# Softmax sums taken another way in the first block, epsilon added as a bias, and attention spread over fewer steps

## The chip, the cores and the metric

The kernel runs on one core of one Trainium2 chip. Its engines are TensorE (PE, with its weight loads shown apart as PEld), VectorE (DVE), ScalarE (ACT), GpSimd (POOL) and SyncE (SP), which here only issues transfers. Each engine works through its own queue in order. The metric is the device time of one execution in microseconds; lower is better.

## The reference

Attention with a soft cap, then a feed-forward layer with a squared ReLU, then a soft mixture of experts. All of it is float32 in the inputs' values, apart from two weight matrices that arrive as float64.

```python
scores = scale * np.matmul(q, k.transpose(0, 1, 3, 2))      # (4, 12, 448, 448)
scores = cap * np.tanh(scores / cap)
scores = scores - np.max(scores, axis=-1, keepdims=True)
attn = np.exp(scores)
attn = attn / (np.sum(attn, axis=-1, keepdims=True) + 1e-09)
x = np.matmul(attn, v)                                      # to (1792, 768)
r = np.maximum(x @ w_in, 0.0)                               # (1792, 2048)
x = (s * (r * r) + b) @ w_out                               # (1792, 768)
logits = x @ phi                                            # (1792, 32)
d = softmax(logits, axis=0); c = softmax(logits, axis=1)
slot_out[e] = np.maximum((d.T @ x)[e] @ w1[e], 0.0) @ w2[e] # 8 experts, 4 slots
out = c @ slot_out
```

## The kernel before

The four batches are four blocks. For each batch, attention is worked out for twelve heads in three groups of four (a quad, `Q` in the code, 0 to 11 over the run), and the result, split into a high and a low part, is the tile `x` of 448 columns that the block's first matrix product (`hidden`, tile `hp`) reads. Scores stand transposed: a chunk is 112 of the 448 key positions on partitions, so a quad has four chunks. One call of `scores` makes the scores of two heads for one chunk (tile `sc`, six matmuls, two PSUM tiles in the first stage and one afterwards) and the tanh into tile `e`; after the second pair of heads `expo` takes the exponential of the whole chunk in place. `e` has three buffers.

The softmax's denominators are sums over partitions, made on PE by a matmul with ones into tile `Sm`; the numerators times `v` go into tile `U`, of which there is one. `finish` takes the reciprocal of the sums, multiplies `U` by it and splits the product into `x`. Constant 1e-9 is scaled by exp(-cap) first, because the maximum is not subtracted where the cap is small enough (the fast branch, which runs here).

Two ways of summing stand beside each other. In the first block (quads 0 to 2, `Q < DIRECT`) all four chunks go through the ones matmul, and a fifth set of four matmuls adds tile `es`, whose partitions 0 to 111 are zero and whose partition 112 holds epsilon (lines 168 and 172). From quad 3 on, DVE adds the four chunks into `es` first (line 158), and only that is summed by matmul, row 112 giving epsilon. GpSimd fills `es` at the start (lines 217 to 222).

`attention` is a generator of 16 steps a quad. Scores are issued on even steps, the other work at fixed steps (`between`, and the four steps of the next quad that end the one before). `run` takes 52 steps of it before any other work (the first stage, up to about 77 us), and then each of the first three blocks takes the 48 steps of the next batch's attention between its own: a block has 48 places, and attention's steps are spread over the first `48 - LEAD` of them (line 671). Meanwhile `convert` turns the float64 weights into float32: a load into one of two `raw` buffers, a scaling copy on ACT, three bit operations on DVE, a store. The last block has no attention; the experts' weights are loaded during it, and the tail after it is paced by those loads. The framework's scheduler may reorder instructions of an engine beyond the order in which the code emits them; a single PSUM tile, tag `T`, is shared in turn by `Sm` (from quad 3 on), `pp`, `tw`, `pf` and `tp`.

## Time and profile before

| | us |
|---|---|
| median of three executions | 686.54 |
| their range | 683.52 to 688.51 |
| the profiled execution | 687.23 |
| its span, first to last instruction | 685.4 |
| PE busy in it | 628.2 (92%) |
| ACT busy | 425.0 (62%) |
| DVE busy | 333.5 (49%) |
| POOL busy | 12.4 (2%) |

The span is shorter than the execution by 1.8 us that lie around the instructions. Busy shares are means over stages that have different limits, so each stage has to be read for itself. The granted PE clock, 1.00 for full speed and 0.50 for half, is 0.98 over the span. Matmuls on float32 data are recorded as two passes each, so that 48 of them in the code are 96 records.

### The profile page before, as it was taken

The numbers are of one execution on the slowest core, as the hardware profiler recorded it, in microseconds if no ns is written. First come the engines' busy times: TensorE is split into PE (matmuls) and PEld (weight loads), VectorE is DVE, ScalarE is ACT, GpSimd is POOL, SyncE is SP. The second block draws the span as 40 slices with busy tenths as digits, with TensorE's granted clock in tenths as the row PEclk, the third lists the DMA queues.
The fourth block names the chain that finished last, engine by engine and source line by source line (L and its number), as shares of the span: only waits on it lengthen the run. The fifth ranks groups of instructions, "written<-read, shape, count | busy, mean of one in ns | idle before, by whom it ended". The sixth has DMA issues, their size and how long they took to land.

```text
span 685.4 us, 11531 instructions
## 1 busy us (share of the span) xinstructions
PE 628.2 (92%) x4714; PEld 395.7 (58%) x4714; DVE 333.5 (49%) x482; ACT 425.0 (62%) x693; POOL 12.4 (2%) x14
## 2 busy tenths in 40 slices
PE   3898999999999899999999999999999988997753
PEld 1333556656566465565665665666868863346643
DVE  6773587896973763555352744534432223111211
ACT  4997889887887776677776777775655551000101
POOL 6000000000000000000000000000000000000000
PEclk9999999999999999999999999999999998998996
DMA  8654367578595532132232221211967629999996
GB/s 250 224 201 119 119 230 266 175 247 280 181 307 192 182 103 81 47 100 74 74 106 63 82 77 63 60 48 45 369 262 286 265 107 403 419 419 418 418 398 212
DMA packets 43724, 136.62 MB, mean 199 GB/s; under 512 B 4352, under 2 KB 21264, under 8 KB 36752
## 3 DMA queue, kind: packets, MB, share of 16 engines
q1 hardware_dynamic: 43376, 135.28, 55.2%
q8 instruction: 39, 0.64, 0.4%
q0 software_dynamic: 288, 0.53, 0.2%
q14 instruction: 21, 0.17, 0.1%
HBM read 117.70 MB, written 18.09 MB: 198 GB/s over the span
## 4 chain that ended last, share of the span: by engine, by line
PE 71%; DMA 12%; ACT 9%; DVE 3%; issue 2%; SPq 0%; DVEq 0%; ACTq 0%
PE hp L438 32%; PE U L189 10%; DMA wt<-in_w_dram 9%; PE sc L115 8%; PE tp L453 4%; ACT e L118 3%; ACT e L153 3%; DMA raw<-in_w_outT_dram 3%; PE hps L732 2%; PE pt L527 2%; PE L L467 2%; PE tw L387 2%; PE pp L369 1%; PE Sm L172 1%; PE si_ps L711 1%
## 5 line engine op out<-in xcount | busy, mean ns | idle before, releaser
L438 PE MATMUL hp<-x,ws 128*128 128x448 f32 x1152 | 278.5, 381 | 0.2 <-ACT ws L422 0.2
L438 PEld LDWEIGHTS hp<-x,ws 128*128 128x128 f32 x1152 | 204.7, 188 | 61.4 <-issue 46.0
L423 DVE TENSOR_TENSOR ws<-wr,ws 128x384 fp32r<-128x384 f32 x128 | 70.6, 554 | 115.3 <-ACT ws L422 114.9
L118 ACT ACTIVATE e<-sc,c_tsc 112x896 f32<-112x896 f32 x96 | 95.9, 1008 | 18.3 <-PE sc L115 17.7
L189 PE MATMUL U<-e,v 112*32 112x448 f32 x768 | 91.0, 542 | 0.2 <-DVE x L75 0.2
L422 ACT CAST ws<-wr 128x384 fp32r<-128x384 f32 x128 | 64.9, 511 | 36.9 <-PE hp L438 36.9
L153 ACT ACTIVATE e<-e,c_acap 112x1792 f32<-112x1792 f32 x48 | 86.2, 1795 | 0.8
L115 PE MATMUL sc<-qh,kh 64*112 64x448 f32 x192 | 46.9, 457 | 13.1 <-DVE kh L74 7.3
L455 ACT COPY g<-tp 112x256 f32<-112x256 f32 x128 | 42.1, 376 | 20.8 <-PE tp L453 20.1
L443 ACT ACTIVATE r<-hp 128x448 f32<-128x448 f32 x64 | 34.6, 540 | 26.9 <-PE hp L438 26.7
L189 PEld LDWEIGHTS U<-e,v 112*32 112x32 f32 x768 | 25.0, 109 | 44.9 <-issue 42.7
L158 DVE TENSOR_TENSOR es<-es,e 112x1792 f32<-112x1792 f32 x18 | 36.4, 2023 | 23.7 <-ACT e L153 23.7
L115 PEld LDWEIGHTS sc<-qh,kh 64*112 64x112 f32 x192 | 18.2, 174 | 46.2 <-issue 22.1
L115 PE MATMUL sc<-ql,kh 64*112 64x448 f32 x192 | 41.5, 384 | 3.2 <-DVE ql L75 3.2
L754 PE MATMUL so_ps<-wt,free 128*32 128x128 f32 x768 | 29.4, 290 | 15.8 <-DMA wt<-in_w_dram 15.8
L775 ACT COPY wt<-op 128x512 f32<-128x512 f32 x12 | 7.0, 586 | 56.7 <-PE op L770 56.7
L115 PE MATMUL sc<-qh,kl 64*112 64x448 f32 x192 | 40.8, 379 | 0.0
L453 PE MATMUL tp<-c_cst,r 128*112 128x128 f32 x256 | 39.0, 275 | 1.3 <-ACT r L444 1.2
L178 DVE RECIPROCAL rec<-rec 128x448 f32<-128x448 f32 x9 | 26.6, 2951 | 24.5 <-ACT rec L177 24.5
L444 ACT ACTIVATE r<-r 128x448 f32<-128x448 f32 x64 | 37.3, 583 | 0.4
L453 PEld LDWEIGHTS tp<-c_cst,r 128*112 128x112 f32 x256 | 29.4, 133 | 11.9 <-ACT g L455 2.4
L754 PEld LDWEIGHTS so_ps<-wt,free 128*32 128x32 f32 x768 | 23.6, 116 | 20.6 <-DMA wt<-in_w_dram 19.6
(141 smaller groups left out, 588.6 us busy)
## 6 DMA issues: line engine op xcount, KB each, us to landing
wt<-in_w_dram SPq DMA_DIRECT2D x48, 1024.0 KB, 15.4
wr<-wsc SPq DMA_DIRECT2D x48, 384.0 KB, 3.1
raw<-in_w_in_dram SPq DMA_DIRECT2D x16, 768.0 KB, 5.2
raw<-in_w_outT_dram SPq DMA_DIRECT2D x16, 768.0 KB, 5.8
wsc<-wr SPq DMA_DIRECT2D x16, 384.0 KB, 3.4
osc<-o SPq DMA_DIRECT2D x24, 256.0 KB, 2.8
wt<-osc SPq DMA_DIRECT2D x6, 1024.0 KB, 7.0
v<-in_v_dram SPq DMA_DIRECT2D x24, 224.0 KB, 3.2
```

What stands on the lines that cost most here:

```text
L115: nc.tensor.matmul(sc[:, i, :S], k[r, c * CP:(c + 1) * CP], q[r, :], start=(n == 0), stop=(n == 2))
L118: nc.scalar.activation(self.e[Q][c][:, 2 * j:2 * j + 2, :], sc[:, :, :S], AF.Tanh, scale=self.c["tsc"][:CP])
L153: self.nc.scalar.activation(e, e, AF.Exp, scale=self.c["acap"][:CP])
L158: self.nc.vector.tensor_add(es, e[0] if c == 1 else es, e[c])
L189: nc.tensor.matmul(self.U[32 * i:32 * i + 32, h, :S], self.v[2 * Q + i // 2][:, i % 2, k * D + 32 * h:k * D + 32 * h + 32], self.chunk(4 * ...
L422: self.nc.scalar.copy(hi, u)
L423: self.nc.vector.tensor_sub(lo, u, hi.bitcast(F32))
L438: nc.tensor.matmul(hp[:, :S], ws[kc // 3][:, w, kc % 3, :], x[:, s, kc, :], start=(k == 0), stop=(k == 3 * KC - 1))
L444: self.mark = nc.scalar.activation(r2, r2, AF.Square).ins
L453: self.nc.tensor.transpose(tp[:CP, q * P:(q + 1) * P], r2[:, q * CP:(q + 1) * CP], self.c["idn"])
L455: self.nc.scalar.copy(self.g[q][:CP, :, fc * P:(fc + 1) * P], tp[:CP, 2 * q * P:2 * (q + 1) * P].rearrange("p (a b) -> p a b", b=P))
L754: nc.tensor.matmul(so_ps[32 * e:32 * e + 32, G, :], ht[G][:, f, 32 * e:32 * e + 32], w2[e // 2][:, e % 2, f, :], start=(f == 0), stop=(f = ...
```

## The change

Epsilon is no longer a row of the summed tile. The sums are copied out of PSUM by an ACT instruction that adds it as a bias, in the first block too, where the reciprocal read PSUM directly; `es` shrinks to 112 partitions and GpSimd fills nothing. In the first block DVE now adds chunks 0 to 2 into `es`, and the matmul with ones runs over `es` and chunk 3 (8 matmuls a quad where there were 20). `U` is accumulated there chunk by chunk, at steps 7, 11 and 15 and at step 3 of the next quad, where it was two chunks at step 9 and two at step 3. `Sm` of the first block moves from a PSUM tile of its own to the shared one. `LEAD` goes from 4 to 10: attention's 48 steps are spread over the first 38 places of a block, not 44.

```diff
--- before.py
+++ after.py
@@ -36,9 +36,9 @@
 EPS = 1e-9
 CAP_FAST = 40.0
 STEPS = 8
-DIRECT = NQ
+LAST = 3
 CASTS = NP
-LEAD = 4
+LEAD = 10
 U = 256
 CU = 768
 XPOS = (1, 4, 7, 10, 13, 15, 15, 15)
@@ -154,29 +154,21 @@
 
     def add(self, Q, c):
 
-        es, e = self.es[:CP], self.e[Q]
-        self.nc.vector.tensor_add(es, e[0] if c == 1 else es, e[c])
-
-    def sums(self, Q, chunks):
+        es, e = self.es, self.e[Q]
+        if c < (LAST if Q < NQ else NCH):
+            self.nc.vector.tensor_add(es, e[0] if c == 1 else es, e[c])
+
+    def sums(self, Q):
 
         nc, c = self.nc, self.c
-        direct = Q < DIRECT
-        if chunks[0] == 0 or not direct:
-            self.Sm = self.psl.tile([P, 512], F32, tag="L", bufs=1, name="Sm") if direct else self.bank("Sm")
-        for k in chunks if direct else ():
+        Sm = self.bank("Sm")
+        parts = [self.es] + self.e[Q][LAST if Q < NQ else NCH:]
+        for n, part in enumerate(parts):
             for i in range(4):
-                nc.tensor.matmul(self.Sm[32 * i:32 * i + 32, :S], c["ones"][:CP, :32], self.chunk(4 * Q + i, k), start=(k == 0), stop=False)
-        if chunks[-1] != NCH - 1:
-            return
-        for i in range(4):
-            nc.tensor.matmul(self.Sm[32 * i:32 * i + 32, :S], c["ones"][:CP + 1, :32], self.es[:CP + 1, i, :], start=not direct, stop=True)
-        rec = self.ap.tile([P, S], F32, tag="rec", bufs=1, name="rec")
-        if Q < NQ:
-            nc.vector.reciprocal(rec, self.Sm[:, :S])
-        else:
-            nc.scalar.copy(rec, self.Sm[:, :S])
-            nc.vector.reciprocal(rec, rec)
-        self.rec = rec
+                nc.tensor.matmul(Sm[32 * i:32 * i + 32, :S], c["ones"][:CP, :32], part[:, i, :], start=(n == 0), stop=(n == len(parts) - 1))
+        self.rec = self.ap.tile([P, S], F32, tag="rec", bufs=1, name="rec")
+        nc.scalar.activation(self.rec, Sm[:, :S], AF.Identity, bias=self.eps)
+        nc.vector.reciprocal(self.rec, self.rec)
 
     def weighted(self, Q, chunks):
 
@@ -214,12 +206,11 @@
         self.prep_pair(0)
         self.prep_pair(1)
         self.load_v(1)
-        self.es = self.ap.tile([P, 4, S], F32, name="es")
-        self.nc.gpsimd.memset(self.es, EPS)
-        if not self.general:
-            self.nc.gpsimd.tensor_scalar(self.es, self.es, self.c["eps"], None, op0=ALU.mult)
-        if DIRECT:
-            self.nc.gpsimd.memset(self.es[:CP], 0.0)
+        self.es = self.ap.tile([CP, 4, S], F32, name="es")
+        self.eps = self.c["eps"]
+        if self.general:
+            self.eps = self.ap.tile([P, 1], F32, name="eps")
+            self.nc.vector.memset(self.eps, EPS)
         last = B * NQ
         for Q in range(last + 1):
             for s in range(2 * STEPS):
@@ -230,13 +221,12 @@
                         if j:
                             self.expo(Q, c)
                     self.between(Q, s)
-                if not self.general and Q and s in (1, 3) and not (s == 1 and Q - 1 < DIRECT):
-                    if s == 1:
-                        self.add(Q - 1, 3)
-                    else:
-                        self.sums(Q - 1, (2, 3))
-                        self.weighted(Q - 1, (2, 3))
-                        self.finish(Q - 1)
+                if not self.general and Q and s == 1:
+                    self.add(Q - 1, 3)
+                if not self.general and Q and s == 3:
+                    self.sums(Q - 1)
+                    self.weighted(Q - 1, (3,) if Q - 1 < NQ else (2, 3))
+                    self.finish(Q - 1)
                 yield
 
     def between(self, Q, s):
@@ -253,17 +243,17 @@
             self.prep_pair(2 * Q + 3)
         if self.general:
             if s == 14:
-                for k in range(1, NCH) if Q >= DIRECT else ():
+                for k in range(1, NCH):
                     self.add(Q, k)
-                self.sums(Q, range(NCH))
+                self.sums(Q)
                 self.weighted(Q, range(NCH))
                 self.finish(Q)
         else:
-            if s == 9:
-                if Q < DIRECT:
-                    self.sums(Q, (0, 1))
+            if Q < NQ and s in (7, 11, 15):
+                self.weighted(Q, (s // 4 - 1,))
+            elif Q >= NQ and s == 9:
                 self.weighted(Q, (0, 1))
-            if s in (9, 13) and Q >= DIRECT:
+            if s in (9, 13):
                 self.add(Q, 1 if s == 9 else 2)
 
     def convert(self, units):
```

What the scheduler makes of it is seen at three places. On PE in the first stage, in quad 2, before (`sc` scores, `Sm` sums, `U` weighted values; the names after the arrow are what is read):

```order
L168 MATMUL Sm<-e,c_ones 32x448 x4
L189 MATMUL U<-e,v 32x448 x8
L115 MATMUL sc<-qh,kh 112x448 x2
L115 MATMUL sc<-ql,kh 112x448
L168 MATMUL Sm<-e,c_ones 32x448 x4
L189 MATMUL U<-e,v 32x448 x8
L115 MATMUL sc<-ql,kh 112x448
L115 MATMUL sc<-qh,kl 112x448 x2
```

The same place after:

```order
L115 MATMUL sc<-qh,kh 112x448 x2
L181 MATMUL U<-e,v 32x448 x16
L115 MATMUL sc<-ql,kh 112x448 x2
L115 MATMUL sc<-qh,kl 112x448 x2
L181 MATMUL U<-e,v 32x448 x8
```

The two sets of sums, each of which stood ahead of scores, are gone from here; `U` still stands inside a group of scores.

On ACT at the end of the first stage, from the second pair of casts of the later quads to the first weight split of block 0, before (L153 is the exponential, L118 the tanh, L74 a cast for a split):

```order
L74 CAST qh<-q_578 128x448
L153 ACTIVATE e<-e,c_acap 112x1792
L118 ACTIVATE e<-sc,c_tsc 112x896 x2
L389 COPY o<-tw 128x512
L153 ACTIVATE e<-e,c_acap 112x1792
L74 CAST qh<-q_661 128x448
L74 CAST kh<-k_662 128x448
L389 COPY o<-tw 128x512
L74 CAST x_385<-U 128x896
```

And after:

```order
L153 ACTIVATE e<-e,c_acap 112x1792
L74 CAST qh<-q_641 128x448
L118 ACTIVATE e<-sc,c_tsc 112x896 x2
L74 CAST kh<-k_642 128x448
L153 ACTIVATE e<-e,c_acap 112x1792
L170 ACTIVATE rec<-Sm,c_eps 128x448
L360 COPY c_tmp<-pp 128x256
L379 COPY o<-tw 128x512
L118 ACTIVATE e<-sc,c_tsc 112x896
L74 CAST x_373<-U 128x896
```

The first exponential of each listing is the last of quad 2. Afterwards the copy of its sums stands behind the next quad's first exponential, with the casts for `q` and `k` ahead of that.

On PE where block 1 starts, before, twelve and more products into its first tiles:

```order
L438 MATMUL hp<-x_1151,ws 128x448 x2
L115 MATMUL sc<-qh,kh 112x448 x2
L115 MATMUL sc<-ql,kh 112x448 x2
L115 MATMUL sc<-qh,kl 112x448 x2
L115 MATMUL sc<-qh,kh 112x448 x2
L115 MATMUL sc<-ql,kh 112x448 x2
L115 MATMUL sc<-qh,kl 112x448 x2
L369 MATMUL pp<-o,c_misc 32x256 x6
```

The like place after is in the last products of block 0, where the scheduler has drawn forward the first scores of block 1's steps:

```order
L115 MATMUL sc<-qh,kl 112x448 x2
L115 MATMUL sc<-qh,kh 112x448 x2
L115 MATMUL sc<-ql,kh 112x448 x2
L115 MATMUL sc<-qh,kl 112x448 x2
L181 MATMUL U<-e,v 32x448
L115 MATMUL sc<-qh,kh 112x448
L359 MATMUL pp<-o,c_misc 32x256 x6
L428 MATMUL hp<-x_373,ws 128x448 x3
```

Two groups of scores stand back to back in both, now in the block before. Over blocks 0 to 2 the products `hp` stand in 135 runs before and 126 after; from block 3 on the rows of PE are the same.

## Rows read from the trace of the kernel before

**Rows 1.** Busy time by stretch: span, PE, PEld, DVE, ACT, POOL, granted clock, DMA share, GB/s.

```profile
12.00:77.00 65.00, 58.76 (x485) 23.09 (x481) 39.38 (x49) 57.73 (x58) 1.36 (x1) 1.00 0.53 179
77.00:212.00 135.00, 132.55 (x830) 82.14 (x829) 105.13 (x135) 111.92 (x169) 0.00 (x0) 1.00 0.71 239
212.00:489.00 277.00, 272.64 (x1730) 173.00 (x1729) 136.36 (x176) 198.40 (x340) 0.60 (x1) 0.99 0.28 92
```

**Rows 2.** Timeline, first 12 us, several engines: start, duration, what, [idle before <-releaser].

```profile
6.68 5.03 POOL L220 TENSOR_SCALAR es<-es,c_eps 128x1792 f32<-128x1792 f32 x1
...
5.18 1.65 DVE L74 CAST qh<-c_tmp 128x448 fp32r<-128x448 f32 x1 [0.59 <-DMA c_tmp<-in_qT_dram]
...
7.04 3.85 DVE L75 TENSOR_TENSOR ql<-c_tmp,qh 128x448 fp32r<-128x448 f32 x1
10.81 0.61 DVE L75 TENSOR_TENSOR kl<-c_tmp,kh 128x448 fp32r<-128x448 f32 x1
...
7.24 0.93 SPq L281 DMA_DIRECT2D raw<-in_w_in_dram  x2
...
7.87 0.56 ACT L74 CAST kh<-c_hh 128x448 fp32r<-128x448 f32 x1 [0.93 <-DMA c_hh<-in_kT_dram]
12.23 1.01 ACT L118 ACTIVATE e<-sc,c_tsc 112x896 f32<-112x896 f32 x1 [3.80 <-PE sc L115]
```

**Rows 3.** Transfers issued in the first 20 us: size, median us to landing.

```profile
raw<-in_w_in_dram SPq DMA_DIRECT2D x2, 768.0 KB, 7.8
```

**Rows 4.** Timeline of ACT, the first stage: first scaling, four idle stretches, one exponential.

```profile
16.98 0.89 ACT L286 ACTIVATE wr<-raw 128x768 f32<-128x768 f32 x1
...
23.79 1.01 ACT L118 ACTIVATE e<-sc,c_tsc 112x896 f32<-112x896 f32 x1 [0.69 <-PE sc L115]
...
46.95 1.91 ACT L118 ACTIVATE e<-sc,c_tsc 112x896 f32<-112x896 f32 x2 [1.35 <-PE sc L115]
...
56.29 1.01 ACT L118 ACTIVATE e<-sc,c_tsc 112x896 f32<-112x896 f32 x1 [1.22 <-PE sc L115]
...
64.72 1.01 ACT L118 ACTIVATE e<-sc,c_tsc 112x896 f32<-112x896 f32 x1 [3.14 <-PE sc L115]
...
70.00 1.80 ACT L153 ACTIVATE e<-e,c_acap 112x1792 f32<-112x1792 f32 x1
```

**Rows 5.** Groups by line, whole span: busy us, mean ns | idle before.

```profile
L168 PE MATMUL Sm<-e,c_ones 112*32 112x448 f32 x96 | 11.5, 551 | 3.0 <-ACT e L153 2.8
L158 DVE TENSOR_TENSOR es<-es,e 112x1792 f32<-112x1792 f32 x18 | 36.4, 2023 | 23.7 <-ACT e L153 23.7
L177 ACT COPY rec<-Sm 128x448 f32<-128x448 f32 x9 | 4.8, 531 | 8.9 <-PE Sm L172 8.9
L485 ACT ACTIVATE c_tmp<-L,c_s 128x448 f32<-128x448 f32 x4 | 2.5, 634 | 4.0 <-PE L L467 4.0
```

**Rows 6.** Timeline, end of the first stage, DVE, ACT and PE.

```profile
73.63 2.96 DVE L175 RECIPROCAL rec<-Sm 128x448 f32<-128x448 f32 x1 [2.86 <-PE Sm L172]
...
77.32 1.09 DVE L199 TENSOR_TENSOR U<-U,rec 128x896 f32<-128x896 f32 x1
...
78.99 0.91 ACT L74 CAST x<-U 128x896 fp32r<-128x896 f32 x1
...
79.93 1.09 DVE L75 TENSOR_TENSOR x<-U,x 128x896 fp32r<-128x896 f32 x1 [0.47 <-ACT x L74]
...
80.37 1.49 PE L438 MATMUL hp<-x,ws 128*128 128x448 f32 x6
...
82.59 2.73 PE L438 MATMUL hp<-x,ws 128*128 128x448 f32 x12
```

**Rows 7.** Timeline of PE, start of block 1: the first of two waits.

```profile
225.12 0.46 PE L115 MATMUL sc<-qh,kh 64*112 64x448 f32 x2 [1.60 <-ACT e L118]
```

**Rows 8.** Busy time by stretch at the same place, columns as in rows 1.

```profile
223.00:228.40 5.40, 2.70 (x22) 1.34 (x24) 5.40 (x6) 4.41 (x4) 0.00 (x0) 0.95 0.42 146
228.40:231.80 3.40, 3.15 (x18) 1.64 (x10) 2.73 (x2) 2.76 (x6) 0.00 (x0) 0.58 0.68 234
```

## The prediction

> **What bounds the kernel now.** I read the busy time by stretch first, then the timeline of the start and of the first stage, then the waits of PE. There are three regimes. From 77 to 489 us (blocks 0 to 2) PE is busy 132.55 of 135 us and 272.64 of 277 us, at a clock of 1.00 and 0.99 [rows 1]: it idles 2.5 and 4.4 us in all, so an edit pays there only by taking work from PE, or one of those few waits. From 12 to 77 us, the first stage, ACT is busy 57.73 of 65 us and PE 58.76 [rows 1]; a busy PE there is partly a PE held back, since scores wait for the tanh that empties their PSUM tile. ACT has four idle stretches before the last exponential of quad 2 at 70.00, of 0.69, 1.35, 1.22 and 3.14 us, 6.4 us together, all released by scores that came late [rows 4]; the scores stood in PE's queue behind sums that waited for an exponential, or behind weighted values. Before 12 us nothing computes but the first splits: the first tanh starts at 12.23, released by PE [rows 2]. The last block and the tail keep their order on PE, and their loads are issued relative to the block's own progress, so what is saved ahead of them reaches the end one for one.
>
> **The start: GpSimd no longer fills es.** The three GpSimd instructions go. On DVE the first cast takes 1.65 us, and the first difference `ql` takes 3.85 us while GpSimd's scaling of `es` runs from 6.68 for 5.03 us; the same operation on the next operand takes 0.61 at 10.81 [rows 2]. I take the overlap for the cause. Without it `ql` is 3.2 us shorter, and the first scores wait for little else. The next limit is ACT itself, whose cast of the second pair's `k`, held by its transfer, ends at 7.87 + 0.56 = 8.43 [rows 2]: the first tanh can come 12.23 - 8.43 = 3.8 us earlier. Soon after, ACT needs the first `raw` of the weights, issued at 7.24 [rows 2] and landing a median 7.8 us later [rows 3], so about 15.0; the scaling that reads it started at 16.98 [rows 4], and no earlier transfer is to be had. With that as the limit 2.0 us are left. Between 2.0 and 3.8 I take 2.8, near the middle, as the first of the two transfers will land ahead of their median and ACT can do a tanh and an exponential first.
>
> [...]
>
> The rows alone leave open whether a first use of an operation is slow, GpSimd or not; then nearly nothing is gained here, which is among the rivals.
>
> **The first stage.** Sums: 36 matmuls fewer (20 to 8 in each of three quads). The old ones are 48 in the code, 96 records, 11.5 us [rows 5], so 0.24 us each and 8.6 us of PE; that alone is worth nothing, as ACT sets the pace. What is worth something is that no sums wait for an exponential ahead of scores, and that `U` now lags its chunk by a whole chunk, so that the four stretches of ACT's idleness, 6.4 us [rows 4], lose their releaser. Against it stand three costs. First, two copies of sums with the bias now run on ACT ahead of the last exponential, 0.53 us each by the copy without one [rows 5], and one small copy, of `pp`, moves behind it: between 0.53 and 1.06 I take 0.7. Second, DVE gets six additions of 2.02 us [rows 5], 12.1 us on top of 39.4 of 65 [rows 1]. It has room, but the copies of `x` on ACT wait for DVE's product with the reciprocal, 2.96 + 1.09 us after the copy of the sums plus what is queued between [rows 6]; ACT has four or five instructions in that time, so I price two such waits at 0.5 us, 1.0 together, with bounds of 0 and 3.0 (a whole addition more in front of each, less what ACT has of its own). An addition is also what frees an `e` buffer, and the tanh of a later chunk queues behind it on ACT; that lies inside the same bound. Third, PE's clock. `U` has one tile, free only after `x` is written, and with the sums gone PE has nothing but scores in that time. At the start of block 1 PE was busy 2.70 of 5.40 us and then ran 3.40 us at a mean clock of 0.58 [rows 8], the nearest row to such a stretch; one drop costs half of 3.4, 1.7 us, if PE has become last. I take one, with bounds of none and two. Together 6.4 - 0.7 - 1.0 - 1.7 = 3.0, between 5.7 and a loss of 0.7.
>
> [...]
>
> The end of the stage stays as long as it was. Before, from 70.00 to 82.59, where the third run of products starts, are 12.6 us [rows 4, 6]. After, the copy of the sums stands behind two tanhs, two casts and the next exponential: by the durations of the same instructions (1.80 for the exponentials, 1.01 for a tanh [rows 4], 0.56 for a cast [rows 2]) 1.80 + 2.02 + 1.12 + 1.80 = 6.7, less the tenths by which ACT's instructions overlap, about 6.1, then 0.53 [rows 5] + 2.96 + 1.09 + 0.91 + 1.09 [rows 6] = 12.7. Before, the reciprocal started earlier but ACT and the in-order scores held the rest. I take the difference for zero. While the sums sit in the shared PSUM tile, `pp` and `tw` stand behind them on PE, with `hp` behind those; that hides in the same 12.7 us.
>
> **Blocks 0 to 2.** Three small terms. The start of block 1 loses 2.70 us to scores that wait for a tanh, of which one wait is 1.60 [rows 7, 8], and 1.7 to the slow clock after them: 4.4. The order afterwards still has two groups of scores back to back, but at the end of block 0, behind products during which ACT has no attention; I take 2.0, with bounds of 0 and 4.4. Runs of `hp` fall from 135 to 126. A run of six takes 1.49 and one of twelve 2.73 us [rows 6], so six in the middle of a run cost 1.24 and a break 0.25; nine fewer are 2.2 at most, and since other small runs appear I take 1.0, with bounds of 0 and 2.2. The bias: nine copies in the later quads become activations; between the copy's 0.531 and the 0.634 of an identity with a scale [rows 5] lies 0.1 us, 0.9 on an ACT that is rarely last, so 0.3 on the path, 0 to 0.9. Against these, attention is denser: 48 steps on 38 places instead of 44, 1.16 times as many in each. ACT is busy 111.92 of 135 us in block 0 [rows 1], 83%, so PE will wait more often. I price it at 1.5 us, about one wait like that of rows 7, with bounds of 0 and 5.4, two stretches like that of rows 8.
>
> **The sum.** -2.8 - 3.0 - 2.0 - 1.0 + 0.3 + 1.5 = -7.0 us. The profiled execution took 687.23 us, its span 685.4 and 1.8 around it; 687.2 - 7.0 = 680.2. That execution lies 0.7 above the median of the three, so 679.5 on the median's scale, 1.0% below 686.54. The three executions lie 5.0 us apart, so about 1% is what a measurement can tell from no change, and the forecast sits on that line.
>
> **The rivals.** (a) The costs in the first stage stay off its path: ACT's stretches close (5.7), no clock drop comes, and with 2.8 at the start and 3.0 in the blocks that makes 11.5, so 675. For it: 6.4 us of idle ACT with one kind of releaser. Against: DVE is loaded to about 51 of some 60 us.
> (b) The change does not do in the first stage what it says: `U` still stands inside a group of scores, PE falls to half its clock in it more than once, and what the sums gave goes into slow scores and waits for additions. Two drops and the whole 3.0 of waits leave a loss of 0.7 there; with 2.8 from the start and the rest cancelling, 686.5 - 2.1 = 684.4. The same time comes if the slow `ql` was not GpSimd's doing, 680.2 + 2.8 - 0.7 = 682.3.
> (c) Slower: in the denser 38 places ACT falls behind, scores hold up PE in its queue, the clock drops, and 2.7 + 1.7 = 4.4 us go each time [rows 8]. Start and first stage bring 5.8; it decides against the change from the second such place on, and three in three blocks with nothing gained back at the old one are 13.2 - 5.8 = 7.4 more: 694. For it: 83% in block 0. Against: ACT is busy 198.40 of 277 us afterwards, 72% [rows 1], and the old density brought one such place.
>
> **How the numbers follow.** Forecast 679.5, reaching from 676 to 682: 0.42, of which somewhat over half lies below 679.7, the line of 1%. (a) 675: 0.24. (b) 682 to 685: 0.28. (c) 694: 0.06. Faster by over 1%: 0.24 + 0.25 = 0.49. Within 1%: 0.17 + 0.28 = 0.45. Slower: 0.06. The outer bounds of all terms give 687 - 17 = 670 and about 692; eight in ten lie between 671.5 and 688.
>
> **What would show it.** The first tanh near 8.5 to 9.5 us and `ql` near 0.6 us; the last exponential of quad 2 near 64 and the third run of `hp` near 76 to 77; ACT's idle time ahead of tanhs in the first stage under 2 us; at most one stretch of half clock there; block 3's first product some 7 us earlier. If the first tanh is early and the first stage no shorter, the waits moved to DVE or to the clock; if PE waits for tanhs in blocks 0 to 2 more than some 7 us, (c) is at work. The forecast is wrong altogether if the last block's loads do not follow its start.

## The result and the profile after

| | before | after |
|---|---|---|
| median, us | 686.24 (682.74 to 691.91, 20 runs) | 678.61 (676.60 to 685.63, 20 runs) |
| ratio after to before | | 0.9908, 95% interval 0.9879 to 0.9936 |
| profiled execution, span, us | 687.23, 685.4 | 681.36, 679.6 |
| granted PE clock over the span | 0.98 | 0.959 |

The changed kernel is 0.9% faster by this ratio, and its interval ends below 1; the two medians alone stand at 0.9889. The forecast was 679.5. The profiled execution before is 1.0 us above its median, the one after 2.8 us above its own, so the two profiles show less than the medians do. In two of the experiments below (`LEAD` back at 4, and PE's waits filled) the longest of the twelve executions lies over 1.5% above the kernel's fastest and is left out of the ratio as slow, and in the second it is the profiled one.

The windows of the changed kernel come first: the three stretches of [rows 1], three short ones in which the clock was low, and blocks 0 to 2 from the third run of `hp` to block 3's first product.

```profile
12.00:77.00 65.00, 52.48 (x403) 20.94 (x401) 49.21 (x55) 56.90 (x59) 0.00 (x0) 0.89 0.58 189
77.00:212.00 135.00, 131.16 (x815) 79.64 (x816) 108.32 (x133) 113.85 (x169) 0.00 (x0) 0.97 0.69 233
212.00:489.00 277.00, 273.93 (x1755) 179.84 (x1755) 131.25 (x177) 197.67 (x348) 0.54 (x1) 1.00 0.31 97
...
37.20:44.00 6.80, 6.50 (x36) 2.62 (x40) 6.80 (x9) 4.53 (x5) 0.00 (x0) 0.53 0.23 71
57.60:64.40 6.80, 5.67 (x32) 2.17 (x36) 6.80 (x6) 5.13 (x7) 0.00 (x0) 0.52 0.33 101
204.40:211.20 6.80, 6.50 (x24) 3.12 (x25) 4.46 (x6) 2.82 (x4) 0.00 (x0) 0.52 0.89 333
...
81.20:478.10 396.90, 390.13 (x2480) 247.38 (x2479) 234.75 (x303) 300.78 (x493) 0.54 (x1) 0.99 0.42 135
```

From 12 to 77 us PE lost 82 records of matmuls and DVE gained 9.8 us of work, but the mean clock there fell from 1.00 to 0.89. Some 13.6 us at half clock stand in two stretches, and a third stands at the end of block 0. This is not one execution's chance: the eight profiled kernels of this study that have the additions show 6.8 to 17.1 us at half clock ahead of the third run of `hp`, the six that keep the direct sums 0 (four of them) or 3.4.

The timeline of the start answers [rows 2] and the first line of [rows 4].

```profile
5.25 0.40 DVE L74 CAST qh<-c_tmp 128x448 fp32r<-128x448 f32 x1 [0.59 <-DMA c_tmp<-in_qT_dram]
...
6.02 0.62 DVE L75 TENSOR_TENSOR ql<-c_tmp,qh 128x448 fp32r<-128x448 f32 x1
...
8.10 0.56 ACT L74 CAST kh<-c_hh 128x448 fp32r<-128x448 f32 x1 [1.14 <-DMA c_hh<-in_kT_dram]
8.57 1.00 ACT L118 ACTIVATE e<-sc,c_tsc 112x896 f32<-112x896 f32 x1
...
14.52 0.90 ACT L276 ACTIVATE wr<-raw 128x768 f32<-128x768 f32 x1 [0.57 <-DMA raw<-in_w_in_dram]
```

`ql` takes 0.62 us where it took 3.85, the cast ahead of it 0.40 where it took 1.65. The first tanh comes 3.66 us earlier, straight behind ACT's cast as forecast, and the first scaling, which waits 0.57 for its transfer, 2.46 us earlier.

The timeline of ACT in the first stage answers [rows 4] and part of [rows 6].

```profile
43.66 1.91 ACT L118 ACTIVATE e<-sc,c_tsc 112x896 f32<-112x896 f32 x2 [2.27 <-PE U L181]
...
63.85 1.01 ACT L118 ACTIVATE e<-sc,c_tsc 112x896 f32<-112x896 f32 x1 [1.64 <-PE U L181]
66.15 1.01 ACT L118 ACTIVATE e<-sc,c_tsc 112x896 f32<-112x896 f32 x1 [1.29 <-PE sc L115]
67.19 1.79 ACT L153 ACTIVATE e<-e,c_acap 112x1792 f32<-112x1792 f32 x1
...
73.28 0.62 ACT L170 ACTIVATE rec<-Sm,c_eps 128x448 f32<-128x448 f32 x1
75.06 0.37 ACT L360 COPY c_tmp<-pp 128x256 f32<-128x256 f32 x1 [1.16 <-PE pp L359]
...
78.00 1.01 ACT L118 ACTIVATE e<-sc,c_tsc 112x896 f32<-112x896 f32 x1 [1.11 <-PE sc L115]
78.91 0.90 ACT L74 CAST x<-U 128x896 fp32r<-128x896 f32 x1
```

Ahead of the last exponential of quad 2 ACT still waits three times for scores, 5.20 us where it was four times and 6.4. Two of the three waits, 3.91 us, have a new releaser: what ended just before these scores on PE is now `U`. ACT has no wait for DVE in this stretch.

The timeline of PE shows the same places from the other side, then the third run of `hp` [rows 6], the end of block 0, where a wait like that of [rows 7] now stands, and the first product into `L` for block 2's last group, whose counterpart before stands last.

```profile
37.25 0.71 PE L115 MATMUL sc<-qh,kh 64*112 64x448 f32 x2 [2.12 <-ACT e L118]
...
40.35 6.31 PE L181 MATMUL U<-e,v 112*32 112x448 f32 x48
...
58.62 0.72 PE L115 MATMUL sc<-qh,kh 64*112 64x448 f32 x2 [2.80 <-ACT e L118]
...
60.57 4.94 PE L181 MATMUL U<-e,v 112*32 112x448 f32 x32
...
81.17 2.71 PE L428 MATMUL hp<-x,ws 128*128 128x448 f32 x12
...
203.05 0.46 PE L115 MATMUL sc<-qh,kh 64*112 64x448 f32 x2 [1.49 <-ACT e L118]
...
204.70 1.70 PE L181 MATMUL U<-e,v 112*32 112x448 f32 x2 [0.80 <-DVE x L75]
...
480.07 0.96 PE L457 MATMUL L<-r,c_hh 128*32 128x448 f32 x8
...
483.60 0.96 PE L467 MATMUL L<-r,c_hh 128*32 128x448 f32 x8
```

The last line is from the trace before: blocks 0 to 2 reach the same product 3.53 us earlier after the change.

`U` of three chunks runs in one piece, 48 records, ahead of the next scores: it had to wait until `x` left its only tile (DVE's last reading of it for `x` ends at 39.74). In the second place the piece has 32. Most of each piece runs at half clock, 3.65 of 6.31 us and 3.83 of 4.94 by the windows above, behind PE's waits for tanhs of 2.12 and 2.80 us.

The groups by line that answer [rows 5]: the sums out of `es` and out of the fourth chunk, the copy with the bias, and the additions.

```profile
L168 PE MATMUL Sm<-es,c_ones 112*32 112x448 f32 x96 | 13.1, 549 | 0.1
L168 PE MATMUL Sm<-e,c_ones 112*32 112x448 f32 x24 | 2.8, 543 | 0.0
...
L159 DVE TENSOR_TENSOR es<-es,e 112x1792 f32<-112x1792 f32 x21 | 42.5, 2024 | 23.9 <-ACT e L153 23.8
...
L170 ACT ACTIVATE rec<-Sm,c_eps 128x448 f32<-128x448 f32 x12 | 7.6, 630 | 4.7 <-PE Sm L168 4.7
```

The copy with the bias takes 0.63 us, 0.10 more than the plain one, as estimated. The sums no longer wait for an exponential: 0.1 us of idle time ahead of them in the whole span.

Stretch by stretch, in the two profiled executions (blocks are told apart by counting the products into `hp`, 288 a block):

| stretch | before, us | after, us | change | forecast |
|---|---|---|---|---|
| start to the first scaling | 16.98 | 14.52 | -2.46 | -2.8 |
| to the last exponential of quad 2 | 53.02 | 52.67 | -0.35 | -3.0 |
| to the third run of `hp` | 12.59 | 13.98 | +1.4 | 0 |
| to block 3's first product | 399.1 | 397.0 | -2.1 | -1.2 |
| block 3's products | 77.3 | 77.3 | 0.0 | 0 |
| from there to the end | 126.4 | 124.2 | -2.2 | 0 |

The last row has the same instructions in both kernels. From block 3's last product to the last matmul, the fourteen profiled executions of this study took 112.4 to 119.1 us, so the 2.2 us of this row lie well within what executions differ by, and single profiles don't divide the 0.9% to better than some 2 us.

### The profile page after: what moved, and what is told of

Same layout as the page of the kernel before. It is cut to its first block, busy times and chain, and to the rows that moved or that the text cites. A ratio compares the mean times of both kernels' runs of the same rounds, so it can differ in the third digit from the quotient of the medians.

```text
span 679.6 us, 11396 instructions
## 1 busy us (share of the span) xinstructions
PE 624.2 (92%) x4642; PEld 400.2 (59%) x4642; DVE 338.1 (50%) x488; ACT 425.7 (63%) x696; POOL 4.1 (1%) x11
## 4 chain that ended last, share of the span: by engine, by line
PE 62%; ACT 15%; DMA 13%; DVE 5%; issue 2%; SPq 0%; ACTq 0%; DVEq 0%
PE hp L428 29%; DMA wt<-in_w_dram 11%; PE U L181 9%; PE sc L115 6%; ACT e L118 5%; ACT e L153 4%; PE tp L443 4%; PE pt L517 2%; DMA raw<-in_w_in_dram 2%; PE L L457 2%; PE tw L377 1%; PE pp L359 1%; PE si_ps L701 1%; ACT ws L412 1%; DVE rec L171 1%
## 5 line engine op out<-in xcount | busy, mean ns | idle before, releaser
L118 ACT ACTIVATE e<-sc,c_tsc 112x896 f32<-112x896 f32 x96 | 96.5, 1014 | 22.2 <-PE sc L115 18.3
L153 ACT ACTIVATE e<-e,c_acap 112x1792 f32<-112x1792 f32 x48 | 86.4, 1799 | 0.8
L159 DVE TENSOR_TENSOR es<-es,e 112x1792 f32<-112x1792 f32 x21 | 42.5, 2024 | 23.9 <-ACT e L153 23.8
L171 DVE RECIPROCAL rec<-rec 128x448 f32<-128x448 f32 x12 | 35.4, 2952 | 29.5 <-ACT rec L170 29.5
L744 PE MATMUL so_ps<-wt,free 128*32 128x128 f32 x768 | 32.4, 324 | 11.4 <-DMA wt<-in_w_dram 11.3
L744 PEld LDWEIGHTS so_ps<-wt,free 128*32 128x32 f32 x768 | 27.2, 130 | 15.2 <-DMA wt<-in_w_dram 13.6
```

Source lines behind the costliest of these rows:

```text
L118: nc.scalar.activation(self.e[Q][c][:, 2 * j:2 * j + 2, :], sc[:, :, :S], AF.Tanh, scale=self.c["tsc"][:CP])
L153: self.nc.scalar.activation(e, e, AF.Exp, scale=self.c["acap"][:CP])
L159: self.nc.vector.tensor_add(es, e[0] if c == 1 else es, e[c])
L171: nc.vector.reciprocal(self.rec, self.rec)
L744: nc.tensor.matmul(so_ps[32 * e:32 * e + 32, G, :], ht[G][:, f, 32 * e:32 * e + 32], w2[e // 2][:, e % 2, f, :], start=(f == 0), stop=(f = ...
```

## The experiments

Two theories stood behind the first four runs. Theory 1: the gain is made in blocks 0 to 2 by the larger `LEAD`, and the first stage nets little. Theory 2: it is made in the first 80 us, by the shorter start and by sums that no longer stand ahead of scores, and `LEAD` is worth nothing. Ratios are to the kernel before, measured beside each on the same chip.

**The lead alone.** The kernel before with one number changed.

```diff
-LEAD = 4
+LEAD = 10
```

> The kernel before with LEAD 10 in place of 4 and nothing else. Theory 1 (the gain is made in blocks 0 to 2, where attention on fewer places leaves the products hp in fewer and longer runs; the first stage gives about 1.4 us net): 5 to 6 us below before, near 681, with hp taking some 7 us less of PE's time between the third run of hp and block 3. Theory 2 (the gain is made in the first 80 us, by the start and by sums that no longer stand ahead of scores; LEAD moves work about): within 1.5 us of before.

Measured: 686.32 us, ratio 0.9999 (0.9964 to 1.0035). Alone it gives nothing, which theory 1 excludes. PE's timeline and the windows show why:

```profile
122.78 0.46 PE L115 MATMUL sc<-qh,kh 64*112 64x448 f32 x2 [2.20 <-ACT e L118]
...
208.45 0.67 PE L438 MATMUL hp<-x,ws 128*128 128x448 f32 x2 [1.90 <-ACT ws L422]
...
124.20:127.60 3.40, 3.40 (x16) 1.03 (x15) 3.40 (x5) 2.84 (x5) 0.00 (x0) 0.55 0.61 192
...
209.50:212.90 3.40, 3.40 (x23) 1.39 (x25) 2.91 (x5) 2.00 (x2) 0.00 (x0) 0.54 0.76 242
```

Runs of `hp` in blocks 0 to 2 fall from 131 to 118, as wanted. The stall at block 1's start [rows 7, 8] is gone, but there are two others, at 123 us inside block 0 and at 208 us at its end, each followed by 3.4 us at half clock: 2.2 and 2.1 us of waits and half of 3.4, some 4 us a place. The first is the mechanism of rival (c), scores that wait for a tanh, close to its price of 4.4. At the second PE waits for a cast of the weights on ACT, so there too ACT is behind, but not through scores.

**The changed kernel with the old lead.**

```diff
-LEAD = 10
+LEAD = 4
```

> The changed kernel with LEAD back at 4, so the bias, the additions and U by the chunk alone. Theory 1: 1 to 3 us below before, near 684.5, with two stretches of half clock in the first 80 us as in the changed kernel. Theory 2: 6 to 8 us below before, near 679.

Measured: 685.57 us, ratio 0.9961 (0.9926 to 0.9996). That is 2.7 us below before by the ratio, inside theory 1's 1 to 3, though not for its reason, since the lead gave nothing alone; theory 2 fails. Half clock in the first stage stands in three stretches, 17.1 us, where theory 1 had two. Blocks 0 to 2 show where the first stage's work went: at block 1's start PE now waits 1.08, 2.12 and 1.10 us for tanhs, and the blocks are 2.6 us longer than before (the table below).

**The bias alone.** The kernel before with epsilon as the bias of the sums' copy and without GpSimd's fills; the first block keeps its direct sums (16 matmuls a quad) and `U` in two halves.

```diff
-        self.nc.gpsimd.memset(self.es, EPS)
...
-            nc.vector.reciprocal(rec, self.Sm[:, :S])
+        nc.scalar.activation(rec, self.Sm[:, :S], AF.Identity, bias=self.eps)
+        nc.vector.reciprocal(rec, rec)
```

> The kernel before with epsilon as the bias of the sums' copy and no fills on GpSimd; the first block still sums all four chunks by matmul in a PSUM tile of its own, U goes two chunks at a time, LEAD is 4. Theory 1: the first tanh comes at 8.6 us and the clock does not fall in the first stage, as PE keeps its sums; so 2 to 3.5 us below before, near 683.5, at least as good as with the additions. Theory 2 in its form that the additions matter: under 1.5 us below before, since scores still stand behind sums there.

Measured: 683.18 us, ratio 0.9952 (0.9918 to 0.9987), as theory 1 had it; its word that the clock would not fall in the first stage was wrong by one stretch of 3.4 us. The additions and `U` by the chunk, on top of it at the same lead, bring nothing that can be measured (0.9961).

**The bias and the lead.** The same with `LEAD` 10.

> The same with LEAD 10: the change without its second part (no additions in the first block, U two chunks at a time). Theory 1: the terms add up, 2 to 3.5 and 5 to 6, so 678 or a little under, no slower than the changed kernel. Theory 2: 3 to 6 us slower than the changed kernel, near 683.

Measured: 682.16 us, ratio 0.9932 (0.9901 to 0.9962). The median is near theory 2's 683, but by the ratios this kernel is only 1.6 us slower than the changed one, not 3 to 6, and the intervals overlap; theory 1's 678 is excluded. Its blocks have the same two stalls as the lead alone (2.08 us at 120, 1.10 and 0.81 at 203 to 205), and 399.8 us. Neither theory holds: at these two leads no part shows a gain by itself except the bias with the fills.

**The fills put back.** The changed kernel with GpSimd's three instructions again at their old place; their values are overwritten and not used.

```diff
         self.es = self.ap.tile([CP, 4, S], F32, name="es")
+        self.nc.gpsimd.memset(self.es, EPS)
+        if not self.general:
+            self.nc.gpsimd.tensor_scalar(self.es, self.es, self.c["eps"][:CP], None, op0=ALU.mult)
+        self.nc.gpsimd.memset(self.es, 0.0)
```

> The changed kernel with GpSimd's two fills and one scaling of the sums' tile put back at their old place (their values are overwritten and not used). Theory 1: GpSimd made ql slow; ql goes back to 3.6 to 3.9 us, the first cast to 1.6, the first tanh to 12, the third run of hp comes 2 to 3 us later, ratio to before 0.994 to 0.995. Theory 2: the start was gained, but waits for U and the slow clock behind it absorb it: ql and the first tanh go back as above, the third run stays within 1 us of 81.2 and the ratio at 0.991. Theory 3 (first use): ql stays at 0.6.

Measured: 681.09 us, ratio 0.9936 (0.9907 to 0.9965). The timeline of its start, its third run of `hp`, and the waits and the window at the end of its block 0:

```profile
5.10 1.59 POOL L211 MEMSET es<- 112x1792 f32 x1 [1.04 <-DVE c_eps L812]
5.29 1.65 DVE L74 CAST qh<-c_tmp 128x448 fp32r<-128x448 f32 x1 [0.59 <-issue]
...
6.79 5.03 POOL L213 TENSOR_SCALAR es<-es,c_eps 112x1792 f32<-112x1792 f32 x1
...
7.15 3.85 DVE L75 TENSOR_TENSOR ql<-c_tmp,qh 128x448 fp32r<-128x448 f32 x1
...
12.35 2.13 ACT L118 ACTIVATE e<-sc,c_tsc 112x896 f32<-112x896 f32 x2 [3.70 <-PE sc L115]
...
84.55 2.71 PE L432 MATMUL hp<-x,ws 128*128 128x448 f32 x12
...
207.32 0.46 PE L115 MATMUL sc<-qh,kh 64*112 64x448 f32 x2 [1.50 <-ACT e L118]
...
208.94 0.94 PE L181 MATMUL U<-e,v 112*32 112x448 f32 x2 [0.76 <-DVE x L75]
...
207.00:214.50 7.50, 6.42 (x40) 3.99 (x41) 6.31 (x9) 5.23 (x9) 0.00 (x0) 1.00 0.79 269
```

With GpSimd back the cast takes 1.65 and `ql` 3.85 us, to the hundredth as before the change, and the third run of `hp` comes 3.4 us later. Theory 1 of this run is right, though the third run moved more than its 2 to 3 us, and a slow first use is ruled out. The order of PE's instructions is the same as in the changed kernel, so nothing but the start was changed; what follows did not stay the same. At the end of block 0 PE waits as it did in the changed kernel (1.50 and 0.76 us for 1.49 and 0.80), but its clock stays at 1.00, where 6.8 us at half clock followed there, and blocks 0 to 2 take 395.0 us for 397.0. Of the 3.4 us at the third run 1.4 are left at block 3's first product. By the ratios the fills cost 0.28% or 1.9 us, within the intervals: that GpSimd delays the start is shown, that the whole kernel gains by it is not clear of noise.

**Filling PE's waits in the first stage.** The changed kernel with six products of `k` and `q` into an unused PSUM tile after the scores of the second and third chunk of quads 1 and 2. They change nothing but PE's activity.

```diff
+                            if not self.general and 0 < Q < NQ and c in (1, 2):
+                                self.warm(2 * Q + j)
...
+        W = self.psl.tile([P, 512], F32, tag="L", bufs=1, name="W")
+        for _ in range(6):
+            self.nc.tensor.matmul(W[:, :S], self.qk[p][2][:, :P], self.qk[p][0], start=True, stop=True)
```

> The changed kernel with 24 extra products of k and q into an unused PSUM tile, six after each of the second and third chunk's scores of quads 1 and 2, where PE waits for a tanh; order and results otherwise the same. Theory 1 (clock): the two stretches of 6.8 us at half clock in the first stage come from these waits and make U (6.31 and 4.94 us) late for the next scores, 2.27 + 1.64 us of ACT idle behind U. Without them the third run of hp starts near 78 (81.2 in the changed kernel), the median is 2 to 3 us lower, ratio to before 0.986 to 0.988, and the executions scatter less. Theory 2 (additions): ACT's waits come from DVE's additions and from U waiting for x whatever the clock; the third run stays at 80 to 81 and the ratio at 0.991.

Measured: 682.41 us, ratio 0.9947 (0.9913 to 0.9980). ACT's timeline and the third run of `hp`:

```profile
41.76 1.91 ACT L118 ACTIVATE e<-sc,c_tsc 112x896 f32<-112x896 f32 x2 [0.22 <-PE U L187]
...
62.10 1.01 ACT L118 ACTIVATE e<-sc,c_tsc 112x896 f32<-112x896 f32 x1 [1.66 <-PE U L187]
65.83 1.01 ACT L118 ACTIVATE e<-sc,c_tsc 112x896 f32<-112x896 f32 x1 [2.71 <-PE sc L115]
...
80.85 2.71 PE L436 MATMUL hp<-x,ws 128*128 128x448 f32 x12
```

The first stretch of half clock is gone: `U`'s 48 records take 4.72 us in place of 6.31, ACT's wait falls from 2.27 to 0.22, and the exponentials that follow come 1.8 us earlier. So that stretch cost about 2 us. The second stays, with `U` at 6.20 us, and ACT waits 4.37 there where it waited 2.93. The third run of `hp` gains 0.3 us. The clock theory holds for the stretch that was removed and doesn't carry the stage. The ratio lies above the changed kernel's, with intervals that overlap. This profile is of the longest of the twelve executions (688.67 us), so what it shows of the blocks, where PE idles 4.3 us more, is not drawn on.

**U in two halves.** The changed kernel with `U` of the first block in two halves again, additions and bias kept.

```diff
-            if Q < NQ and s in (7, 11, 15):
-                self.weighted(Q, (s // 4 - 1,))
-            elif Q >= NQ and s == 9:
+            if s == 9:
                 self.weighted(Q, (0, 1))
```

> The changed kernel with U of the first block's quads in two halves (chunks 0 and 1, then 2 and 3, as before the change) instead of by the chunk; additions and bias kept. Theory 1: U waits for x in either form and PE thins out in the same places; half clock in the first stage stays at 10 us or more and the ratio at 0.991. Theory 2: the burst of three chunks of U ahead of scores, 6.31 us, is what makes ACT wait; with two chunks at most in a burst the third run of hp comes 1 to 2 us earlier and the ratio is 0.988 to 0.989.

Measured: 681.25 us, ratio 0.9951 (0.9916 to 0.9986). ACT's waits for scores between the first scaling and quad 2's last exponential are 0.91, 2.28 and 3.82 us, 7.0 in all, with 10.2 us at half clock: shorter pieces of `U`, no shorter waits. Theory 1 has the clock right. The ratio lies above both numbers, with an interval that reaches down to 0.9916.

**A larger lead.** The changed kernel with `LEAD` 16, then 22 (six executions each).

```diff
-LEAD = 10
+LEAD = 16
```

> The changed kernel with the lead at 16: 48 steps of attention on 32 places instead of 38. If a denser attention costs (rival c of the prediction), PE waits for tanhs in blocks 0 to 2 grow from some 6.6 us of idle by 4 or more and the ratio rises to 0.997 to 1.003. If the lead gains by whole runs of hp, as theory 1 of the first runs had it, a further 2 to 3 us are gained, ratio 0.987 to 0.988. If the lead is worth next to nothing, the ratio stays at 0.990 to 0.992.

Measured: 672.76 us, ratio 0.9808 (0.9769 to 0.9846), far below every expectation. The windows of blocks 0 to 2, and of the place where the changed kernel stalls:

```profile
77.00:212.00 135.00, 132.46 (x847) 82.14 (x845) 109.98 (x136) 113.16 (x170) 0.00 (x0) 1.00 0.68 230
212.00:480.00 268.00, 266.68 (x1712) 172.38 (x1712) 131.59 (x174) 197.49 (x341) 0.54 (x1) 1.00 0.30 97
203.00:216.00 13.00, 12.96 (x79) 7.81 (x78) 8.50 (x11) 9.64 (x15) 0.00 (x0) 1.00 0.71 250
```

No half clock is left in blocks 0 to 2 (the first stage has 17.1 us of it), and between 203 and 216 us PE idles 0.04 us. Attention of a batch now ends so far ahead of its block that PE has no wait for scores or for `x` where blocks 0 and 1 meet.

> The changed kernel with the lead at 22: 48 steps of attention on 26 places. If attention that ends well ahead of its block is what pays (no wait for x and scores where two blocks meet), the gain is complete at 16 and the ratio stays at 0.980 to 0.983. If ACT cannot follow a denser attention, PE's waits for tanhs in block 0 grow from 0.4 us to 5 or more and the ratio rises to 0.985 or above.

Measured: 677.33 us, ratio 0.9861 (0.9819 to 0.9903). By the ratio the gain is past its best, though the two intervals overlap. The ratio is that of the second case, but the waits for tanhs in block 0 are 2.0 us and not 5; all of PE's idle time there is 4.5 us in place of 2.3, and more runs of `U` (46 for 34) break up the products.

**The lead of 16 without the other edits.** First with the bias alone, then with nothing else.

> The kernel before with the epsilon as a bias of the sums' copy, without GpSimd's fills, and the lead at 16; the first block's sums stay eight direct products of each exponential and U stays in two halves. If the additions and U by the chunk bring nothing of their own, the ratio is that of the changed kernel at the same lead, 0.979 to 0.983. If they pay only with a larger lead, as the first runs hinted (the changed kernel 0.9908, bias and lead 10 alone 0.9932), the ratio is 0.986 to 0.990.

Measured: 678.45 us, ratio 0.9878 (0.9842 to 0.9913).

> The kernel before with nothing changed but the lead, 16. If the lead pays by itself from some value between 10 and 16 on, the ratio is 0.984 to 0.987 (the 3 to 4 us of bias and fills are missing against bias_lead16). If it pays only beside the other edits, 0.995 to 1.000, as with a lead of 10.

Measured: 678.95 us, ratio 0.9883 (0.9840 to 0.9926). From some value between 10 and 16 on the lead pays by itself, 1.2%: its interval lies wholly below that of the lead of 10. The ratio is a little above the first case of its expectation, because bias and fills bring nothing that shows beside this lead (0.9878 against 0.9883): the third run of `hp` comes 3.4 us earlier with them, at 79.8 for 83.2, but the blocks then take 396.2 us for 390.8. The additions with `U` by the chunk seem to be worth 0.7%, 0.9808 against 0.9878, by intervals that just touch. The profiles don't bear that out: block 3 starts at 472.7 us with all edits, 476.0 with the bias and 474.0 with the lead alone, and most of the remaining distance lies in the tail (112.4 us for 118.5 and 118.9), whose instructions none of them changes.

**Filling the waits at the lead of 16.** As above, with twelve products after the third chunk.

> The changed kernel with the lead at 16 and 36 extra products into an unused PSUM tile: six after the second and twelve after the third chunk's scores of quads 1 and 2. In its order U of the first three chunks splits into 16 and 8 products with a group of scores between. Theory 1 (clock): without the extra products the first stage at this lead has 17.1 us at half clock (3.4 + 6.8 + 6.8) and the third run of hp starts at 82.2. If slow U is what ACT waits for there, less than 4 us at half clock remain, the third run starts at 77.5 to 79.5 and the ratio falls from 0.981 to 0.976 or below. Theory 2: ACT waits for U held by x whatever the clock, as with 24 extra products, where 6.8 us less at half clock left the third run at 81; third run 81 to 82.5, ratio 0.980 to 0.984.

Measured: 680.52 us, ratio 0.9886 (0.9853 to 0.9918). The third run of `hp` starts at 82.69 us. PE's and ACT's timelines at quad 2:

```profile
59.98 4.91 PE L187 MATMUL U<-e,v 112*32 112x448 f32 x32 [2.08 <-DVE x L75]
...
65.52 0.57 ACT L74 CAST kh<-k 128x448 fp32r<-128x448 f32 x1 [3.95 <-PE sc L115]
```

The longer filling also changed the order: `U` now stands ahead of the whole group of scores, PE waits 2.08 us for `x`, and ACT idles 3.95 us behind it. Half clock in the first stage fell from 17.1 to 6.8 us and the stage got no shorter, as theory 2 had it: `U` in its one tile, held by `x`, stands in front of scores. What each of the two causes is worth is not separated by this run, since 3.4 of the 4.91 us of this `U` still ran at half clock. The ratio lies above both forecasts; the blocks' order of work is that of the lead of 16, but PE idles 7.5 us in them for 3.6, in waits for converted weights and scores that the experiment was not made to explain.

All fourteen profiled executions in blocks 0 to 2, from the third run of `hp` to block 3's first product. "Work" is an estimate: the time less PE's idle time and less half of the time at half clock; the tail is from block 3's last product to the last matmul:

| kernel | us | PE idle | at half clock | work | tail | ratio |
|---|---|---|---|---|---|---|
| before | 399.1 | 6.8 | 3.4 | 390.6 | 116.9 | 1 |
| lead 10 alone | 400.8 | 9.3 | 6.8 | 388.1 | 119.1 | 0.9999 |
| bias | 398.0 | 6.3 | 3.4 | 390.0 | 114.2 | 0.9952 |
| bias, lead 10 | 399.8 | 8.7 | 6.8 | 387.7 | 116.9 | 0.9932 |
| all, lead 4 | 401.7 | 10.2 | 6.8 | 388.1 | 113.7 | 0.9961 |
| all, lead 10 (after) | 397.0 | 6.8 | 6.8 | 386.8 | 115.5 | 0.9908 |
| after, fills back | 395.0 | 7.6 | 0 | 387.4 | 117.9 | 0.9936 |
| after, PE's waits filled | 401.5 | 11.1 | 6.8 | 387.0 | 117.4 | 0.9947 |
| after, `U` in halves | 398.6 | 8.7 | 3.4 | 388.2 | 113.9 | 0.9951 |
| all, lead 16 | 390.5 | 3.6 | 0 | 386.9 | 112.4 | 0.9808 |
| bias, lead 16 | 396.2 | 7.9 | 0 | 388.3 | 118.5 | 0.9878 |
| lead 16 alone | 390.8 | 4.4 | 0 | 386.4 | 118.9 | 0.9883 |
| all, lead 22 | 394.9 | 6.3 | 0 | 388.6 | 114.5 | 0.9861 |
| all, lead 16, waits filled | 394.5 | 7.5 | 0 | 387.0 | 114.7 | 0.9886 |

From before to after the blocks gained by less work on PE (390.6 to 386.8), not by fewer waits: PE's idle time is the same and the time at half clock doubled. From the lead of 10 to that of 16, with all edits, it is the other way round, with equal work, 3.2 us less idle time and no half clock. All five kernels with a lead of 16 or 22 are free of half clock here, and of the nine with 4 or 10 only one. Idle time and half clock are two things: three of the rows without half clock idle over 7 us.

## Why the prediction was right

The time came out 0.9 us below the forecast and well inside its range, but not step by step: the start was right, the first stage was put far too high, and the blocks too low.

**The start** was right in mechanism and size: 2.46 us at the first scaling for 2.8, its limits ACT's cast and then the `raw` transfer, as named. The fills put back show that GpSimd was the cause: with them the first cast takes 1.65 us and `ql` 3.85, without them 0.40 and 0.62. How it delays them is not shown. With GpSimd's scaling running from 6.79 for 5.03 us, `ql` ends at 11.00, before the scaling does, and two other DVE instructions that run beside it take no longer than in the changed kernel: the cast of `kh` 0.37 us at 6.86 (0.40 there), `kl` 0.61 at 10.92 (0.62).

**The first stage** is the step that failed: "Together 6.4 - 0.7 - 1.0 - 1.7 = 3.0". It gave 0.35, at the low end of its bounds, and the end of the stage, put at zero, cost 1.4 more. The four idle stretches of ACT were not closed; 5.2 of 6.4 us came back, 3.9 of them with `U` as their releaser. Of the costs set against them, the copies took about 0.9 (two of 0.62 less the small one's 0.37) for 0.7, and the waits for DVE, priced at 1.0, did not come. The step took for granted that `U`, lagging a whole chunk, would stay out of the scores' way. In fact its one tile is held until `x` is written, so three chunks of it gather into one piece ahead of the next scores. The clock fell twice for 6.8 us, where one stretch of 3.4 was priced; filling PE's waits showed 2 us for the first of them. The sign "at most one stretch of half clock there" was wrong, and "the third run of `hp` near 76 to 77" came at 81.17. At the end of the stage the copy of the sums stands 6.1 us behind the exponential, as worked out, but the copy of `x`, ready to go when DVE's product ends at 78.1, starts at 78.91 behind a tanh that had itself waited 1.11 us for scores. Rival (b) described the stage up to the third run of `hp` correctly, with a loss of 0.7 for the 1.0 measured; what it missed lies further on.

**Blocks 0 to 2** gave 2.1 for 1.2 in the profiled execution. The stall at block 1's start was to shrink by 2.0 of its 4.4; it moved to the end of block 0 instead (1.49 + 0.80 us of waits, then 6.8 us at half clock) and gave nothing. The same two waits stand at the same place in three more profiles of kernels with the additions and a lead of 10, followed by 6.8, 3.4 and 0 us at half clock, so what this place costs is partly chance. Fewer runs of `hp` gave more than the 1.0 taken: 131 fell to 121, and PE was busy with these products for 206.8 us where it was 209.6. The denser attention, priced at 1.5, cost nothing here (PE idle 6.8 us in both), but did cost a stall in block 0 in both kernels that had the lead of 10 without the additions. That the additions and `U` by the chunk pay only beside the larger lead, if they do, agrees with this: they change the order of PE's instructions at the boundary and in block 0, and the stall at 120 to 123 us is absent. That is read from four traces, not shown by an experiment of its own, and the difference, 0.9908 against 0.9932, lies inside the intervals.

**The sum** was right because the errors offset each other, and that is luck: the forecast was too high by 2.7 us in the first stage, by 1.4 at its end and by 0.3 at the start, and too low by 0.9 in the blocks and by 2.2 in the tail. By the ratio, 0.9908 of 686 is -6.3 us (-8.3 to -4.4), by the medians -7.6, against -7.0. Block 3's first product came 3.5 us earlier, not 7 (the prediction also set that place at 489 us; by count it is 481.7 before and 478.1 after). Its lower outer bound took 17 us off where its own bounds for the terms add up to 16.1. The tail's 2.2 us stand in unchanged instructions. An earlier start of block 3 is not what shortens the tail: the kernels that start it earliest after the lead of 16, at 474.0 and 476.0 us, have tails of 118.9 and 118.5, two of the three longest. So they are best taken for scatter, and so is a part of what the lead of 16 shows, whose blocks are 8.6 us shorter than before while its median is 12.5 us lower.

## What to carry to other kernels

Take a producer out of an engine's queue only after asking what will stand in its place: here sums made room, and weighted values held by a single tile moved in, behind which ACT waited 2.27 and 1.64 us. Where PE is nearly full, count the places where it waits and then runs at half clock: with the lead alone such a place cost some 4 us, and a change of order that only moves it gained nothing. Price such a place from several profiles, as the same waits were followed by 6.8 us at half clock in one and by none in another. A number like `LEAD` is worth trying at values well past the first: 10 alone gave nothing, 16 alone 1.2%. Before constants are filled on an idle GpSimd, look at what VectorE does meanwhile: here three GpSimd instructions delayed the first tanh by 3.8 us (12.35 for 8.57).

## What was not expected of the hardware

A GpSimd fill that only writes `es` slowed a VectorE cast with one input from 0.40 to 1.65 us. The cast takes that time before the change (fill from 4.99 for 1.59 us, cast from 5.18) and again with the fills put back (5.10 and 5.29); with the lead alone, where the fills are also in place, the first tanh comes as late as before, at 12.16 us (lead 10) and 12.19 (lead 16).

The same instructions don't get the same clock in each execution. Of the twenty executions of the changed kernel, the eleven with a mean clock of 0.972 to 0.985 took 676.6 to 679.0 us and the nine with 0.957 to 0.965 took 680.5 to 685.6; the profiled one, at 0.959, is of the second group. In the tail, where PE waits for loads time and again (seven waits, 11.3 us in all, in the changed kernel), the half-clock stretches up to the last matmul add up to anything from 3.4 to 27.3 us over the fourteen profiles, and the tail takes 112.4 to 119.1 us. That this is why executions of one kernel lie 7 to 13 us apart in most of the runs is likely but not shown, as each kernel was profiled once; effects of 2 us stayed open after twelve executions each.
